# Attention and S4D layers on one core: kernel powers in ten double-buffered batches, scaled on GpSimd, with the step sizes first

## The chip, the cores and the metric

The kernel runs on one core of a Trainium2 chip. The metric is the device time of one execution in microseconds (us). A core has four compute engines that matter here: PE (TensorE, matrix products), DVE (VectorE), ACT (ScalarE) and POOL (GpSimd). SP (SyncE) issues most DMAs; POOL issues some. Each engine executes its own queue in order and waits on semaphores for the others.

## The reference

Four layers are applied to x (2048 tokens by 640 channels), alternately self-attention with 32 heads of 20 channels and a long convolution (S4D), each on the normalized x and added to it. Both attention layers share their weights, and so do both convolutions.

```
x = x + attention(layernorm(x), wqkv, wo)
x = x + s4d(layernorm(x), ...)
x = x + attention(layernorm(x), wqkv, wo)
x = x + s4d(layernorm(x), ...)

# the convolution kernel of s4d, for 640 channels d, 128 states n, 2048 positions l
dt = exp(log_dt)                              # the step sizes, one per channel
A  = -exp(log_A_real) + 1j * A_imag
C  = (C_real + 1j * C_imag) * dt[:, None]
P  = exp((A * dt[:, None])[:, :, None] * pos)
K  = 2 * einsum("dn,dnl->dl", C, P).real
y  = causal_convolution(u, K) + u * D_skip    # by FFT
```

## The kernel before

**Stages.** `seq` runs the layers. The first attention layer has two stages. A head stage (L664 to L748) loads the tokens in four groups of four blocks (`xr`), normalizes them (`ln_stats`, then L720 on ACT), transposes them on PE into two halves of half precision (`xh`, `xl`), and makes the first block of queries and keys (`block0`) and the first values (`values4`). Then the score loop (`scores`, `values`) runs 1024 times in a layer: PE computes a 128x1024 tile S (L769), ACT takes its exponential into `pt` (L772), and PE multiplies `pt` with the values V into `pa` (L786). The remaining queries, keys and values are computed beside it on PE (`jobs`, L560), and DVE empties the PSUM tiles `m` of those into `qc`. A plan with estimated costs (`Plan`, `slot`, `fill`, `weave`) decides while the program is written where each of these jobs stands between the scores.

**The convolution kernel.** `kgen` is a generator whose steps are woven into the first attention layer. It needs the powers of exp(A dt) at twelve exponents (LV, from 1 to 1536). First come the loads of `lar`, `aim`, `cr` and `ci` (128 states by 640 channels), then the step sizes: `ldt` is loaded as 128x5 (`k_d5`), `exp_exact` takes a polynomial exponential on DVE with one step on ACT, the result goes to DRAM (`dtd`) and comes back on all partitions (`k_dt`). `exp_exact` also runs on all of `lar` (128x640). DVE multiplies the four tiles by `k_dt`.

`powers(k)` then handles 128 channels, five times, in one set of the buffers `ks_`, `kc_` and `ke`. ACT makes 12 scaled copies of `aim` (L216); DVE reduces them to one turn and takes the absolute value (c); ACT takes two sines (L227, L229) and 12 exponentials of the scaled `lar` (L225); DVE multiplies cosine and sine by the exponential, and SP stores both to `wd` in DRAM. ACT must load another function table for a change between sine, exponential and square root; the order of the functions alternates between batches (`"esc"`, `"sce"`), so that like functions meet.

After the last batch `kgen` yields `"hold"`. Its second half gives the memory of the powers' buffers to new tiles (`ktab`, `kneg`), loads 32 channels of powers at a time back from `wd` (`kpw`, a DMA issued by POOL), expands them on DVE (`expand`, `left`, `right`), contracts them on PE (L322) and stores the kernel to `kd`.

**Order.** In the head stage a compile-time scheduler places the instructions: of those that are ready by its own estimates, each engine takes the one that was written first. The steps of `kgen` up to `"hold"` are written after the head stage, so they are placed where its work leaves an engine free. From the score loop on, `plan.keep` ties all matrix products, and the calls of DVE and the DMA issues of POOL and SP that go through `Ordered` (L74), to the order in which they are written. The engines execute the resulting queues in that fixed order. Nearly all of the calls on DVE, POOL and SP are recorded at line L74, that of the helper.

**Weights.** `stage` loads a slice of `wqkv` and returns `make`, which multiplies it by 256 and splits it into a half-precision part `wh` and its remainder `wl`, both on DVE. With `pool` given (the first block's weights `b0`, `b1` and the values' `b0`, `b1`, `b2`) it is used in the head stage. The second attention layer runs the same code with x already on the chip.

## Time and profile before

| what | us |
|---|---|
| median of 3 runs | 2904.78 (2903.93 to 2905.59) |
| profiled execution | 2906.51 |
| its span | 2904.6 |
| busy PE, ACT, DVE, POOL | 2581.2, 2360.6, 1497.7, 795.5 |
| first normalization on ACT (L720) | at 16.46 |
| first scaled copy of the powers (L216) | at 67.00 |
| first exponential of the scores (L772) | at 119.83 |
| second layer: first L720, first L772 | at 1606.27, at 1687.01 |

The profile records one execution. Times are in us from the start of its span. A line of a timeline has the start, the duration, the engine and the line of code, the operation, output and inputs with their shape, a count, and in brackets how long the engine had been idle before and what ended that. SPq and POOLq lines are DMA issues. A line of the stretches has the length, then the busy time of PE, of weight loads, DVE, ACT and POOL with the number of instructions, the granted clock of PE as a share of full speed, the DMA share and GB/s.

### The profile page before, as it was taken

To read this page: it belongs to the slowest core of one execution; us is meant where nothing else is said; L and a number is where in the kernel's file an instruction comes from. 1 tells how busy PE (TensorE), PEld (TensorE's weight loads), DVE (VectorE), ACT (ScalarE), POOL (GpSimd) and SP (SyncE) were. 2 spreads that over 40 slices of the span, in tenths; PEclk is the share of its full clock that TensorE was granted. 3 is DMA by queue.
4 is the path that set the end of the run, shared out by engine and by line. 5 is a ranking of instruction groups with operands and counts; after the bars stand their busy time and mean duration, and the time that the engine had idled before them with its cause. 6 is when DMAs were issued, how large, how long until landed. Compare 5 with 4: busy or idle time off the path is not lost.

```text
span 2904.6 us, 127995 instructions
## 1 busy us (share of the span) xinstructions
PE 2581.2 (89%) x57088; PEld 1537.6 (53%) x57088; DVE 1497.7 (52%) x3333; ACT 2360.6 (81%) x2862; POOL 795.5 (27%) x1229
## 2 busy tenths in 40 slices
PE   7679898998999788789999898999999978878999
PEld 3235555554555444367788554544444433334988
DVE  8555667777775687146777633332222200001865
ACT  5878888998899788855565488999999989998364
POOL 1002223222222222330067012222222332222376
PEclk9889999999999999999999999999999999999999
DMA  5212222222111111335454212121211211112265
GB/s 165 105 55 58 62 59 60 62 53 68 52 55 42 51 41 50 131 119 185 190 188 140 67 35 64 55 65 40 61 46 44 66 28 39 31 43 61 86 204 162
DMA packets 174754, 231.45 MB, mean 80 GB/s; under 512 B 35952, under 2 KB 124336, under 8 KB 172400
## 3 DMA queue, kind: packets, MB, share of 16 engines
q1 hardware_dynamic: 139856, 180.84, 19.2%
q0 software_dynamic: 34336, 42.32, 5.8%
q8 instruction: 450, 7.37, 1.1%
q14 instruction: 112, 0.92, 0.1%
HBM read 150.94 MB, written 72.10 MB: 77 GB/s over the span
## 4 chain that ended last, share of the span: by engine, by line
ACT 26%; PE 18%; issue 6%; DMA 3%; DVE 2%; POOL 1%; SPq 0%; ACTq 0%; POOLq 0%; DVEq 0%
ACT pt L772 25%; PE psv L1135 2%; PE psy L1145 2%; PE po L1041 2%; PE psx L1123 2%; PE psx L1100 2%; PE pst L1110 1%; PE pkf L1015 1%; PE pkx L998 1%; PE pv L524 1%; PE po L1035 1%; PE pa L786 1%; PE pq L682 1%; DMA kl<-kd 1%; PE pkt L1007 1%
## 5 line engine op out<-in xcount | busy, mean ns | idle before, releaser
L772 ACT ACTIVATE pt<-S 128x1024 f32<-128x1024 f32 x2048 | 1932.4, 1040 | 168.2 <-PE S L769 155.1
L786 PE MATMUL pa<-pt,V 64*32 64x512 f32 x16384 | 1144.3, 597 | 17.3 <-DVE oc L74 9.3
L769 PE MATMUL S<-qop,kop 61*32 61x512 f16 x16384 | 921.8, 383 | 184.6 <-ACT pt L772 149.1
L769 PEld LDWEIGHTS <-kop 61*32 61x32 f16 x16384 | 393.8, 90 | 836.9 <-issue 742.5
L786 PEld LDWEIGHTS pa<-pt,V 64*32 64x32 f32 x16384 | 330.1, 107 | 93.7 <-issue 32.0
L74 POOL DMA_DIRECT2D dn<-oc x256 | 126.2, 499 | 446.2 <-DVE oc L74 352.4
L74 POOL DMA_DIRECT2D ot<-oc x256 | 129.2, 512 | 392.5 <-DVE oc L74 313.3
L74 DVE TENSOR_SCALAR qc<-m 128x512 f32<-128x512 f32 x64 | 44.2, 690 | 298.9 <-PE m L560 298.8
L322 PE MATMUL m<-kb,ka 64*32 64x64 f32 x10240 | 158.4, 222 | 44.6 <-issue 42.4
L322 PEld LDWEIGHTS m<-kb,ka 64*32 64x32 f32 x10240 | 150.8, 105 | 82.4 <-issue 65.3
L74 DVE COPY oc<-pa 128x512 f32<-128x512 f32 x64 | 44.2, 691 | 275.0 <-PE pa L786 275.0
L74 POOL DMA_DIRECT2D db<-dn x256 | 128.5, 508 | 133.7 <-DMA dn<-dr 126.0
L74 DVE TENSOR_TENSOR kb<-ktab 128x512 f32<-128x512 f32 x240 | 155.9, 684 | 16.4 <-PE m L322 16.4
L560 PE MATMUL m<-xh,wh 64*32 64x512 f16 x2560 | 148.8, 382 | 12.5 <-DVE qc L74 12.5
L560 PE MATMUL m<-xl,wh 64*32 64x512 f16 x2560 | 148.0, 381 | 0.0
L560 PE MATMUL m<-xh,wl 64*32 64x512 f16 x2560 | 147.0, 380 | 0.2 <-issue 0.2
L560 PEld LDWEIGHTS <-wh 64*32 64x32 f16 x5120 | 97.1, 94 | 79.0 <-issue 42.2
L1128 POOL TENSOR_TENSOR t<-t,kb 128x512 f32<-128x512 f32 x80 | 101.9, 1274 | 71.2 <-DVE t L74 70.3
L1112 ACT COPY xt<-pst 128x1024 f16<-128x1024 f16 x80 | 81.6, 1023 | 46.7 <-PE pst L1110 46.5
L74 DVE TENSOR_SCALAR dr<-dr 128x16 f32<-128x16 f32 x64 | 14.7, 229 | 188.5 <-DMA dr<-dn 188.4
L74 DVE TENSOR_TENSOR oc<-oc,db 128x512 f32<-128x512 f32 x64 | 44.1, 690 | 125.7 <-DMA db<-dn 124.2
L74 POOL DMA_DIRECT2D dn<-dr x64 | 35.6, 556 | 263.8 <-DVE dr L74 256.7
(222 smaller groups left out, 3877.3 us busy)
## 6 DMA issues: line engine op xcount, KB each, us to landing
ka<-kha SPq DMA_DIRECT2D x80, 256.0 KB
kb<-khb SPq DMA_DIRECT2D x80, 256.0 KB
db<-dn POOLq DMA_DIRECT2D x256, 64.0 KB, 2.6
qop<-qs SPq DMA_DIRECT2D x256, 40.0 KB
kop<-ks SPq DMA_DIRECT2D x128, 80.0 KB
ot<-oc POOLq DMA_DIRECT2D x256, 40.0 KB, 2.0
otl<-ot SPq DMA_DIRECT2D x32, 320.0 KB
kha<-kn SPq DMA_DIRECT2D x20, 512.0 KB
```

Source lines behind the costliest of these rows:

```text
L74: made = f(out, *a, **k)
L322: chain(te.matmul(ps[r][32 * j:32 * j + 32, c8, :], a[n // 2][rows, ch, :], b[n][rows, dd, :], start=(n == 0), stop=(n == 3), tile_positio ...
L560: chain(te.matmul(ps[r][32 * t:32 * t + 32, :], a_[rows, ct, 32 * t:32 * t + 32], m[rows, ct, sl], start=(k == 0), stop=(k == 14), tile_po ...
L769: chain(te.matmul(S[32 * t:32 * t + 32, 512 * r:512 * r + 512], kt_[rows, kc + 32 * t:kc + 32 * t + 32], qt[rows, :], start=True, stop=Tru ...
L772: se.activation(pt, S, AF.Exp, scale=SCALE)
L786: chain(te.matmul(pa[r][32 * j:32 * j + 32, :], V[rows, kt, VP * h:VP * h + 32], pts[j // 2][rows, 512 * (j % 2):512 * (j % 2) + 512], sta ...
L1041: te.matmul(pos[hf], oh[:, ct, :], m[:, ct, 320 * hf:320 * hf + 320], start=False, stop=(ct == NCT - 1 and m is wol))
L1100: te.matmul(ps[:, r, i, :], e1[:, e, s, r, :], m[:, s, bs], start=(n == 0), stop=(n == 2))
L1112: se.copy(xt, pt.rearrange("p k g c -> p k (g c)"))
L1123: te.matmul(px, f2[:, f, :], xt[:, k, :], start=(n == 0), stop=(n == 2))
L1128: ge.tensor_mul(t2, t2, kb)
L1135: te.matmul(pv[:, g].rearrange("p r i c -> p (r i c)"), t1[:, g * P:g * P + P], fa, start=True, stop=True)
```

## The change

1. The step sizes' exponential, with its load and store, is written ahead of everything else, in a pool of its own; `kgen` only loads `k_dt`.
2. `lar`'s exponential is one ACT step in place of `exp_exact`.
3. `powers` handles 64 channels (BA), ten times, with two sets of buffers. The multiplications by the twelve exponents, for `aim` and now also for `lar`, run on POOL (24 of 128x64 a batch); ACT takes one wide exponential and two sines. `tie` keeps ACT's functions of successive batches in the written order.
4. `kpw` becomes two tiles of their own that do not reuse the powers' memory. The first two are loaded right behind batch 0, and later ones a batch further ahead.
5. In `stage`, `wh` of the head stage's weights moves from DVE to ACT, and the calls of `make` move behind the normalization of the first group.
6. The tokens of a group are loaded before the group ahead of it is handled; the first group's loads stand ahead of the weights', the selection matrix's behind them.

The core of the diff (the constants' lines and unchanged context are left out):

```
+    with tc.tile_pool(name="dt", bufs=1) as dp:
+        d5 = dp.tile([P, D // P], F32, name="k_d5")
+        sy.dma_start(d5, ldt.rearrange("o (p c) -> (o p) c", c=D // P))
+        exp_exact(dp, d5, D // P)
+        sy.dma_start(dtd.rearrange("o (p c) -> (o p) c", c=D // P), d5)
...
     def kgen():
-        BA, BC, DC = 128, 32, 8
+        BA, BC, DC = 64, 32, 8
...
+        kpw = [kp.tile([P, 2, BC, NL], F32, name=f"kpw{n}") for n in range(2)]
...
-            d5 = kx.tile([P, D // P], F32, name="k_d5")
-            sy.dma_start(d5, ldt.rearrange("o (p c) -> (o p) c", c=D // P))
-            exp_exact(kx, d5, D // P)
-            sy.dma_start(dtd.rearrange("o (p c) -> (o p) c", c=D // P), d5)
             sy.dma_start(dt, dtd.partition_broadcast(P))
             yield
-            exp_exact(kx, ld["lar"])
+            se.activation(ld["lar"], ld["lar"], AF.Exp)
...
-        kw1 = tc.tile_pool(name="kw1", bufs=1, side="right")
+        act = [None]
+        kw1 = tc.tile_pool(name="kw1", bufs=2, side="right")
...
             for n, v in enumerate(LV):
-                se.activation(s[:, :, n], ld["aim"][:, bs], AF.Copy, scale=v)
+                ge.tensor_scalar_mul(s[:, :, n], ld["aim"][:, bs], v)
+            for n, v in enumerate(LV):
+                ge.tensor_scalar_mul(e[:, :, n], ld["lar"][:, bs], v)
...
                 if f == "e":
-                    for n, v in enumerate(LV):
-                        se.activation(e[:, :, n], ld["lar"][:, bs], AF.Exp, scale=v)
+                    act[0] = tie(se.activation(e, e, AF.Exp), act[0])
                 elif f == "s":
-                    se.activation(s, s, AF.Sin, scale=TWO_PI)
+                    act[0] = tie(se.activation(s, s, AF.Sin, scale=TWO_PI), act[0])
                 else:
-                    se.activation(c, c, AF.Sin, scale=-TWO_PI, bias=hpi)
+                    act[0] = tie(se.activation(c, c, AF.Sin, scale=-TWO_PI, bias=hpi), act[0])
...
+            if k == 0:
+                for n in range(2):
+                    load_powers(n)
...
         def load_powers(k):
-            w = p2.tile([P, 2, BC, NL], F32, name="kpw")
-            ge.dma_start(w, wd[:, :, k * BC:k * BC + BC, :].rearrange("r p d n -> p r d n"))
-            return w
+            ge.dma_start(kpw[k % 2], wd[:, :, k * BC:k * BC + BC, :].rearrange("r p d n -> p r d n"))
...
-        cur = load_powers(0)
-        yield from expand(0, cur, tab, neg)
-        cur = load_powers(1)
+        yield from expand(0, kpw[0], tab, neg)
+        load_powers(2)
...
             if k + 1 < NE:
-                yield from expand(k + 1, cur, tab, neg)
-                if k + 2 < NE:
-                    cur = load_powers(k + 2)
+                yield from expand(k + 1, kpw[(k + 1) % 2], tab, neg)
+                if k + 3 < NE:
+                    load_powers(k + 3)
...
-                ve.tensor_scalar_mul(wh, wt, WS)
+                if pool:
+                    se.activation(wh, wt, AF.Copy, scale=WS)
+                else:
+                    ve.tensor_scalar_mul(wh, wt, WS)
...
+            coming = load_x(0)
             for i4 in range(4):
...
+                xr = coming
                 if i4 == 0:
+                    made_ = [stage(n * D, P, f"b{n}", wb[n], hp) for n in range(2)]
                     sy.dma_start(self_, c_sel)
-                    made_ = [stage(n * D, P, f"b{n}", wb[n], hp) for n in range(2)]
+                if i4 < 3:
+                    coming = load_x(i4 + 1)
...
-                if i4 == 0:
-                    for make in made_:
-                        make()
...
                     se.activation(t, xr[i], AF.Identity, scale=rs[:, i:i + 1], bias=nb[:, i:i + 1])
                     xn.append(t)
+                if i4 == 0:
+                    for make in made_:
+                        make()
```

More of the change, by code (lines that the diff above doesn't have):

```diff
@@ L156, in rstd, with exp_exact @@
         return rs
-    def exp_exact(pool, xx, n=D):
+    def exp_exact(pool, xx, n):
         k, r, q, z = (pool.tile([P, n], F32, name=f"ee_{t}{n}") for t in "krqz")
@@ L691, in values4, with load_x @@
                         pass
-            for i4 in range(4):
-                if x is None:
-                    xr = []
-                    for i in range(4):
-                        t = xp.tile([P, D], F32, tag=f"xr{i}", name=f"xr{i}")
-                        sy.dma_start(t, xv[:, 4 * i4 + i, :])
-                        xr.append(t)
-                else:
-                    xr = [x[:, 4 * i4 + i, :] for i in range(4)]
+            def load_x(i4):
+                if x is not None:
+                    return [x[:, 4 * i4 + i, :] for i in range(4)]
+                ts = [xp.tile([P, D], F32, tag=f"xr{i}", name=f"xr{i}") for i in range(4)]
+                for i, t in enumerate(ts):
+                    sy.dma_start(t, xv[:, 4 * i4 + i, :])
+                return ts
+            coming = load_x(0)
+            for i4 in range(4):
+                xr = coming
                 if i4 == 0:
+                    made_ = [stage(n * D, P, f"b{n}", wb[n], hp) for n in range(2)]
                     sy.dma_start(self_, c_sel)
-                    made_ = [stage(n * D, P, f"b{n}", wb[n], hp) for n in range(2)]
+                if i4 < 3:
+                    coming = load_x(i4 + 1)
                 if stats is None:
@@ L708, in attention @@
                     mv, rs = stats(i4)
-                if i4 == 0:
-                    for make in made_:
-                        make()
-                    made_ = [stage(2 * D + q * QW, QW, f"b{q}", [w[:, :, q * QW:q * QW + QW] for w in wv], hp)
-                             for q in range(NQ)]
-                    ve.tensor_copy(sel, self_)
                 xn = []
@@ L721, in attention @@
                     xn.append(t)
+                if i4 == 0:
+                    for make in made_:
+                        make()
+                    made_ = [stage(2 * D + q * QW, QW, f"b{q}", [w[:, :, q * QW:q * QW + QW] for w in wv], hp)
+                             for q in range(NQ)]
+                    ve.tensor_copy(sel, self_)
                 for ct in range(NCT):
```

## The prediction

> **What bounds the kernel now.** I read the page, then the busy time by stretches, then the timelines of ACT, DVE and SyncE up to 260 us, and last the same stage of the second attention layer, into which nothing else is woven.
>
> ```profile
> span 2904.6 us, 127995 instructions
> ...
> L772 ACT ACTIVATE pt<-S 128x1024 f32<-128x1024 f32 x2048 | 1932.4, 1040 | 168.2 <-PE S L769 155.1
> ```
>
> The exponentials on ACT (L772) pace both attention layers. They were kept waiting for 168.2 us in all, so it matters where that idle time lies.
>
> ```profile
> 118.50:175.60 57.10, 25.37 (x432) 9.23 (x432) 30.40 (x53) 40.28 (x76) 1.51 (x2) 0.67 0.25 95
> 175.60:250.00 74.40, 71.92 (x2099) 39.06 (x2090) 33.48 (x60) 73.77 (x79) 14.19 (x28) 1.00 0.14 42
> ```
>
> The columns are the length, then the busy time of PE, weight loads, DVE, ACT and POOL, then the granted clock. From 175.6 us ACT is busy 73.77 of 74.40 us. In the 57.1 us before, PE has 25.37 us of work at a granted clock of 0.67, and POOL has 1.51. The timeline of ACT tells what happens there:
>
> ```profile
> 16.46 3.36 ACT L720 ACTIVATE xr<-xr,nb,rs 128x640 f32<-128x640 f32 x4 [6.47 <-DVE nb L74]
> ...
> 67.00 0.66 ACT L216 ACTIVATE ks__1093<-k_aim 128x128 f32<-128x128 f32 x2 [1.40 <-DVE k_ci L74]
> ...
> 119.83 1.02 ACT L772 ACTIVATE pt<-S 128x1024 f32<-128x1024 f32 x1
> ...
> 173.77 1.02 ACT L772 ACTIVATE pt<-S 128x1024 f32<-128x1024 f32 x1 [13.90 <-PE S L769]
> 175.59 48.31 ACT L772 ACTIVATE pt<-S 128x1024 f32<-128x1024 f32 x51 [0.80 <-PE S L769]
> ```
>
> The first exponential runs at 119.83 us, and by 175.59 only 18 have run (the first and the last of them are shown). The last two batches of powers sit between them. Then DVE stops everything:
>
> ```profile
> 155.00 0.32 DVE L74 MEMSET ktab<- 128x96 f32 x2 [4.01 <-DMA wd<-kc__1236]
> 159.50 0.42 DVE L74 COPY ktab<-kpw 128x192 f32<-128x192 f32 x2 [4.19 <-DMA kpw<-wd]
> ...
> 170.21 0.68 DVE L74 TENSOR_SCALAR qc<-m 128x512 f32<-128x512 f32 x1
> ```
>
> In the loop DVE keeps the written order. It waits 4.01 us for the last store of the powers (wd), 4.19 us for the first load back (kpw), expands until 170.21, and only then empties the PSUM banks (qc) for which PE, and behind PE the scores, wait. So the powers set the start of steady running, not the attention's own preparation. The second layer shows that stage without them:
>
> ```profile
> 1606.27 4.17 ACT L720 ACTIVATE xn<-x,nb,rs 128x640 f32<-128x640 f32 x5
> ...
> 1674.45 0.30 ACT L530 ACTIVATE V<-pv 128x160 f32<-128x160 f32 x1 [1.73 <-DVE V L74]
> 1676.49 0.30 ACT L530 ACTIVATE V<-pv 128x160 f32<-128x160 f32 x1 [1.73 <-DVE V L74]
> ...
> 1687.01 33.60 ACT L772 ACTIVATE pt<-S 128x1024 f32<-128x1024 f32 x36 [0.78 <-DMA qop<-qs]
> ```
>
> There 36 exponentials take 33.60 us (0.933 each) from the very first. Eighteen would take 16.8 us, so the 19th, now at 175.59, could run at 119.83 + 16.8 = 136.6: the loop holds 39.0 us of stall. The stage ahead has slack too: from normalization to first exponential it takes 1687.01 - 1606.27 = 80.7 us there and 119.83 - 16.46 = 103.4 us here. Part of that is more work: a token block's values take 1676.49 - 1674.45 = 2.04 us there for 320 columns; for the first layer's 480 I estimate 3.06, over 16 blocks 16 us more. The other 103.4 - 80.7 - 16 = 6.7 us are disturbance.
>
> **The change, part by part.** *Head of the stage.* Between the root of the variance and nb, DVE casts weights:
>
> ```profile
> 9.78 0.20 ACT L150 ACTIVATE lt<-va 128x4 f32<-128x4 f32 x1 [7.76 <-DVE va L74]
> ...
> 16.27 0.15 DVE L74 SCALAR_TENSOR_TENSOR nb<-mv,rs 128x4 f32<-128x4 f32 x1
> ```
>
> The root is there at 9.98. Six small steps of some 0.15 us with nothing between would bring nb to 10.9, 5.4 us earlier. The step sizes' exponential now runs first: 17 DVE steps of five columns, at most 17 x 0.15 = 2.6 us, part of it before the first tokens land; I charge 1.4. Its load and store stand ahead of later loads on SyncE's queue; if the store's wait holds tokens up, the lower bound below covers it. So 4 us are won, with bounds 0 and 6. Five casts go from DVE to ACT, behind the normalization; two of them precede the first q and k products, which I leave inside these bounds. The tokens a group ahead I cost at nothing: their buffers are double already, and what covers them is the matrix work of the group before. Of the 6.7 us of disturbance I take 3 as gone (bounds 0 and 7), since twelve long DVE steps of the exact exponential leave the stage. First exponential: 119.8 - 7 = 113, bounds 107 and 120.
>
> *Start of the powers.* They need the step sizes on all partitions (k_dt), and lar and aim:
>
> ```profile
> 15.95 0.63 SPq L74 DMA_DIRECT2D k_aim<-in_aim  x1
> ...
> 59.77 0.32 SPq L74 DMA_DIRECT2D k_dt<-dtd  x1
> ```
>
> k_dt is loaded at 59.77, and the first scale runs at 67.00. With that chain done near 10 us, what is late next is lar and aim, issued at about 16, and two DVE steps that give way to the layer's own work. With some 4 us to land (the wait after the last wd store is of that size) and as much again until DVE is free, POOL could begin at 25; I take 29, with bounds 22 and 67 (nothing won).
>
> *Length of the powers.* Now 67.00 to 155.00: 88 us for five batches, 17.6 each. The prices:
>
> ```profile
> L225 ACT ACTIVATE ke<-k_lar 128x128 f32<-128x128 f32 x60 | 16.1, 432 | 0.4 <-DVE kc__1128 L74 0.4
> ...
> L227 ACT ACT_TABLE_LOAD x5 | 6.4, 1283 | 3.3 <-DVE kc__1128 L74 1.9 <-DVE kc__1236 L74 1.0 <-DVE kc__1164 L74 0.4
> ...
> L227 ACT ACTIVATE ks__1093<-ks__1093 128x1536 f32<-128x1536 f32 x1 | 1.5, 1484 | 0.0
> ```
>
> Per 128 channels ACT now runs 24 narrow steps (16.1 / 60 = 0.268 each, as they overlap), 6.4 us, then two sines of 1.5 and two table loads of 1.28: 12.0 us. After it: three wide passes, 4.5 us cut in two with a little overhead, 4.9, and again two table loads, since one batch's order is sines first and the next one's exponential first: 7.5 us. That frees 22 us of ACT over the five. Here the Trainium skill speaks against smaller batches: "ScalarE: Activation LUTs", section What ACT_TABLE_LOAD costs, puts a switch of set at 2.66 us, a drain included. By that the ten switches would cost 27 us and not 13, but every switch in this trace shows the load of 1.283 and the next step right behind, so I go by the row.
>
> POOL gets 24 multiplications of 128x64 per batch, 240 in all, written at a stride. No POOL row is that step; the nearest are:
>
> ```profile
> L925 POOL CAST woh<-wot 128x640 fp32r<-128x640 f32 x10 | 7.0, 715 | 6.9 <-DMA wot<-in_wo 5.4 <-DMA qop<-qs 1.5
> ...
> L74 POOL MEMSET V<- 128x128 f32 x6 | 2.1, 344 | 0.0
> ```
>
> Ten times the columns take 0.715, and twice the elements, strided, 0.344. I take 0.25 us, nearest to the second, with bounds 0.1 and 0.7. At 0.25 a pair of batches has 12 us of POOL, beside the other engines, as the second set of buffers lets POOL run one batch ahead. The pair's period is then the chain of one buffer: half the POOL work of a batch (3), reduction on DVE (2), ACT (5), products (2), store (4), 16 us if nothing queues and two batches share it. With the layer's own work in between I take 17, and 5 x 17 = 85 us. ACT has the room:
>
> ```profile
> 1606.00:1720.00 114.00, 103.19 (x1312) 62.21 (x1316) 57.00 (x129) 71.87 (x109) 2.64 (x5) 0.97 0.20 58
> ```
>
> Of these 71.87 us, 33 are exponentials, so the stage's own share of ACT is 39 us; with wider values and five casts some 48, of which about 10 lie before 29 us. From 29 to 113 that leaves 84 - 38 = 46 us for 5 x 7.5 = 38. So the powers end at 29 + 85 + 4 for the last store = 118, bounds 105 and 160, and the last batch or so falls beside the first exponentials.
>
> *Into the loop.* kpw has buffers of its own and is loaded after batch 0, so the 4.19 us go; the multiplications queued behind these two loads on POOL wait for a store (4 us, one time), covered by the batch already scaled. From memset to steady running it was 175.59 - 155.00 = 20.6, less 4.2 leaves 16.4. Powers: 118 + 16.4 = 134.4. Attention: 113 + 16.8 = 129.8. The later one holds: the 19th exponential comes at 134.4 instead of 175.6, 41 us earlier. Behind it the written order is the same, and the loads a batch further ahead only widen a cover that is there (kpw is waited for once). In the second layer the same casts move from DVE to ACT and behind the normalization, which ACT did first there already: nothing, bounds -2 and +2. I take 2 off for steps that the in-order queues hold up, and get 39.
>
> Sum: 2904.6 - 39 = 2865.6 of span; the profiled execution took 2906.51 against a span of 2904.6, and the median is 2904.78, so 2866 stands for the median.
>
> **The rivals.** *The powers still trail into the loop.* If queues of three engines in fixed order leave three of ten batches at the first exponential, each costs there what two batches of twice the size cost between 119.83 and 155.00, 35 us, by four: 8.8 us. 113 + 26 + 4 + 16.4 = 159.4, a gain of 16: 2889. For it speaks that ACT has only 46 - 38 = 8 us to spare.
>
> *The start does not move.* If k_dt's load stays where it is on SyncE's queue, the powers run from 67 for 85 us, end at 152 + 4, and the loaded kpw alone is won: 3 us and 7 from the head that nobody waits for. 2902, within 0.2%, about what a measurement of this kernel can tell from no change. Against it: nothing of the layer stands ahead of that chain any more.
>
> *POOL becomes the bound.* 240 steps of p from 29 us, and 12 behind for the last batch: the break-even is 29 + 240 p + 12 = 159, at p = 0.49 us. At 0.65, as for a step whose cost is all fixed, the end is 197, the 19th exponential at 213, and the time 2904.8 + 38 = 2943. A steady theft of POOL's port by DVE would do it as well:
>
> ```profile
> L1128 POOL TENSOR_TENSOR t<-t,kb x80: 1264/1274/1284, 1469.7 to 2886.2; 128x512 f32<-128x512 f32 x80
> ```
>
> All 80 stay within 1264 and 1284 ns beside a working DVE, so I see no theft. The Trainium skill, "GPSIMD Engine Reference", section Key points, has DVE steps with two SBUF inputs contend with GpSimd, which would be this case.
>
> **How the numbers follow.** Forecast 0.62; trailing powers 0.17; start unmoved 0.07; POOL as the bound 0.08; better than forecast 0.06 (powers by 105, first exponential by 107, 19th at 124: 2853). Faster takes the forecast, the trailing and the better case, and a third of the unmoved start: 0.87. Within 0.2%: 0.05. Slower: 0.08. The range goes from 2850, below the better case, to 2892, past the trailing one, and leaves out the last two rivals.
>
> **What would show it.** Right: in the changed profile the first POOL multiplication lies at 25 to 35 us and takes 0.2 to 0.35; the first L772 lies at 107 to 118; the memset of ktab does not wait past 120; the copy from kpw waits for no DMA; L772's idle time falls by over 20 us, and PE's clock is full from 120 on. Wrong: POOL busy without a gap up to the memset, an exponential still followed by 14 us of idle ACT, or a first normalization later than 16.

## The result, and the profile after

The changed kernel takes 2952.25 us (median of 4 runs, 2950.21 to 2955.98) against 2904.36 us of the kernel before on the same chip: a ratio of 1.0163, 95% interval 1.015 to 1.0176. It is slower by 48 us, where 39 us of gain were forecast. The profiled execution has a span of 2950.8 us, 46.2 more than before. The page after:

```profile
span 2950.8 us, 128213 instructions
...
PE 2584.5 (88%) x57088; PEld 1538.6 (52%) x57088; DVE 1483.2 (50%) x3334; ACT 2350.8 (80%) x2773; POOL 904.7 (31%) x1469
...
L785 ACT ACTIVATE pt<-S 128x1024 f32<-128x1024 f32 x2048 | 1932.9, 1040 | 156.9 <-PE S L782 143.6
```

The exponentials are now at L785. They take what they took (1932.9 us) and wait 156.9 us instead of 168.2. So the score loop lost nothing; the loss lies ahead of it. ACT's timeline at the same places as before:

```profile
18.14 3.35 ACT L727 ACTIVATE xr<-xr,nb,rs 128x640 f32<-128x640 f32 x4 [5.49 <-DVE nb L74]
...
203.15 2.85 ACT L785 ACTIVATE pt<-S 128x1024 f32<-128x1024 f32 x3
207.05 1.02 ACT L785 ACTIVATE pt<-S 128x1024 f32<-128x1024 f32 x1 [1.05 <-PE S L782]
208.57 22.46 ACT L785 ACTIVATE pt<-S 128x1024 f32<-128x1024 f32 x24 [0.49 <-PE S L782]
```

The first exponential runs at 203.15 us, 83.3 later than before. From there the loop runs nearly without a hole: the 19th is the 15th of the 24 that begin at 208.57, so it starts at 208.57 + 14 x 0.936 = 221.7, which is 46.1 after the 175.59 of before. That is the whole difference of the spans. DVE at the start of the kernel's second half:

```profile
205.64 0.14 DVE L74 MEMSET ktab<- 128x96 f32 x1 [2.70 <-DMA wd<-kc__1414]
205.80 0.25 DVE L74 COPY ktab<-kpw 128x192 f32<-128x192 f32 x1
...
216.54 0.68 DVE L74 TENSOR_SCALAR qc<-m 128x512 f32<-128x512 f32 x1
```

The copy from `kpw` waits for no DMA, as forecast, and the first `qc` comes 10.9 us behind the memset instead of 15.2. But the memset, which waits for the last store of the powers, runs at 205.64 instead of 155.00. POOL's timeline tells what the powers were waiting for:

```profile
47.46 5.42 POOL L220 TENSOR_SCALAR ks__1080<-k_aim 128x64 f32<-128x64 f32 x12 [24.50 <-DVE k_ci L74]
52.96 6.09 POOL L222 TENSOR_SCALAR ke<-k_lar 128x64 f32<-128x64 f32 x12
...
79.78 7.05 POOL L222 TENSOR_SCALAR ke<-k_lar 128x64 f32<-128x64 f32 x12 [8.48 <-DVE ks__1080 L74]
...
153.87 4.98 POOL L220 TENSOR_SCALAR ks__1341<-k_aim 128x64 f32<-128x64 f32 x12
164.84 0.44 POOL L74 PARTITION_ALL_REDUCE k2m<-k  x1 [5.99 <-issue]
172.45 0.47 POOL L222 TENSOR_SCALAR ke<-k_lar 128x64 f32<-128x64 f32 x1 [7.17 <-issue]
...
190.87 7.11 POOL L222 TENSOR_SCALAR ke<-k_lar 128x64 f32<-128x64 f32 x12
```

Each line is a run of up to twelve multiplications. It begins at 47.46 (29 forecast), takes 5.0 to 7.1 us per twelve (3.0 forecast), and ends at 197.98. The 240 steps fill 116.7 us of these 150.5. Of the rest, 4.3 us are POOL's two loads of `kpw`, its transfers of `qm` and the all-reduce; 15.5 us are three waits for a buffer that DVE still uses (8.48 is shown, the others are 2.67 and 4.33); and 13.2 us stand around the all-reduce with nothing to wait for ("issue", 5.99 and 7.17). On the other side of the hand-over, DVE stands at the first step that reads a set:

```profile
64.14 0.56 DVE L74 TENSOR_SCALAR kc__1118<-ks__1119 128x768 f32<-128x768 f32 x1 [9.03 <-POOL ks__1119 L220]
123.97 0.56 DVE L74 TENSOR_SCALAR kc__1229<-ks__1230 128x768 f32<-128x768 f32 x1 [9.15 <-POOL ks__1230 L220]
180.15 0.56 DVE L74 TENSOR_SCALAR kc__1377<-ks__1378 128x768 f32<-128x768 f32 x1 [10.50 <-POOL ks__1378 L220]
```

There are ten such waits, one per batch, of 4.55 to 10.50 us, 72.5 us in all. DVE's queue is in order, so the layer's own work stands behind them, and PE behind that: one of ACT's copies into V follows 18.58 us of idle time, ended by DVE's, and from 170 to 200 us PE is busy 1.19 of 30 us at a granted clock of 0.50 (the figure behind the length, and the one behind POOL's count):

```profile
159.71 0.30 ACT L538 ACTIVATE V<-pv 128x160 f32<-128x160 f32 x1 [18.58 <-DVE V L74]
```
```profile
170.00:200.00 30.00, 1.19 (x16) 0.54 (x17) 6.02 (x8) 5.94 (x7) 23.76 (x52) 0.50 0.15 55
```

### The profile page after: what moved, and what is told of

Same layout as the page of the kernel before. It is cut to its first block, busy times and chain, and to the rows that moved or that the text cites. A ratio compares the mean times of both kernels' runs of the same rounds, so it can differ in the third digit from the quotient of the medians.

```text
span 2950.8 us, 128213 instructions
## 1 busy us (share of the span) xinstructions
PE 2584.5 (88%) x57088; PEld 1538.6 (52%) x57088; DVE 1483.2 (50%) x3334; ACT 2350.8 (80%) x2773; POOL 904.7 (31%) x1469
## 4 chain that ended last, share of the span: by engine, by line
ACT 24%; PE 20%; issue 5%; DMA 2%; DVE 2%; POOL 1%; SPq 0%; POOLq 0%; ACTq 0%; DVEq 0%
ACT pt L785 23%; PE psv L1148 2%; PE psy L1158 2%; PE psx L1136 2%; PE pa L799 2%; PE psx L1113 2%; PE po L1054 2%; PE pv L532 1%; PE pst L1123 1%; PE pkf L1028 1%; PE S L782 1%; PE pkx L1011 1%; PE pq L690 1%; PE po L1048 1%; DMA kl<-kd 1%
## 5 line engine op out<-in xcount | busy, mean ns | idle before, releaser
L785 ACT ACTIVATE pt<-S 128x1024 f32<-128x1024 f32 x2048 | 1932.9, 1040 | 156.9 <-PE S L782 143.6
L74 DVE TENSOR_TENSOR kb<-ktab 128x512 f32<-128x512 f32 x240 | 155.6, 681 | 16.4 <-PE m L328 16.4
L532 PE MATMUL pv<-wv,xh 128*128 128x480 f16 (+1 forms) x320 | 86.1, 357 | 42.8 <-DVE V L74 36.3
L532 PEld LDWEIGHTS <-xh 128*128 128x128 f16 x800 | 70.1, 100 | 92.9 <-issue 71.7
```

Source lines behind the costliest of these rows:

```text
L74: made = f(out, *a, **k)
L532: chain(te.matmul(ps[:, :n], a_[:, ct, sl], m[:, ct, :], start=(k == 0), stop=(k == 14)))
L785: se.activation(pt, S, AF.Exp, scale=SCALE)
```

## The experiments

The first theory read these rows as a matter of order: a compile-time queue that puts DVE's read of a set, and POOL's all-reduce behind the sets, ahead of the attention's own preparation. Its rivals were the amount of POOL's work, whatever the order, and steps of POOL and DVE that slow each other. Fourteen kernels were run. This table collects them. They ran on several chips, so the ratio, which is to the kernel before on the same chip, compares them better than the medians do; the memset is that of `ktab`, and the last column is the span of the profiled execution less the time of the memset.

| kernel | median us | ratio (95%) | first exponential | memset | span - memset |
|---|---|---|---|---|---|
| before | 2904.36 | 1 | 119.83 | 155.00 | 2749.6 |
| after | 2952.25 | 1.0163 (1.015 to 1.0176) | 203.15 | 205.64 | 2745.2 |
| act_scales | 2894.51 | 0.9966 (0.9954 to 0.9979) | 120.88 | 154.29 | 2744.7 |
| pool_alone | 2970.96 | 1.0213 (1.0192 to 1.0234) | 167.21 | 222.18 | 2748.2 |
| head_alone | 2892.19 | 0.9964 (0.9949 to 0.998) | 121.16 | 141.50 | 2743.5 |
| dve_alone | 2894.01 | 0.9969 (0.9958 to 0.998) | 117.39 | 147.56 | 2743.7 |
| dve_wide | 2878.81 | 0.9914 (0.99 to 0.9928) | 122.39 | 138.55 | 2738.4 |
| dve_wide_oldhead | 2880.70 | 0.992 (0.9906 to 0.9935) | | | |
| pool_wide | 2898.72 | 0.9981 (0.9971 to 0.999) | 153.06 | 155.55 | 2741.3 |
| pool_idle_work | 2961.52 | 1.0199 (1.0182 to 1.0216) | 189.90 | 223.31 | 2732.8 |
| pool_idle_four | 2906.48 | 0.9998 (0.9986 to 1.0011) | 128.42 | 161.82 | 2746.0 |
| order_tied | 2944.51 | 1.0143 (1.0102 to 1.0185) | 138.48 | 201.15 | 2742.2 |
| pool_half | 2936.30 | 1.0099 (1.0068 to 1.0129) | 147.45 | 191.76 | 2746.0 |
| no_all_reduce | 2938.26 | 1.0106 (1.0085 to 1.0126) | 173.12 | 200.09 | 2742.4 |
| pool_half_three | 2918.17 | 1.0047 (1.003 to 1.0064) | 135.26 | 168.15 | 2746.5 |
| after_early | 2944.64 | 1.0126 (1.0108 to 1.0144) | 197.51 | 200.00 | 2738.8 |

The last column is the main finding. The memset moves over a range of 85 us, and what follows it stays between 2738 and 2750 us, but for one kernel. The first exponential shows no such tie: order_tied has it 65 us earlier than the changed kernel, and the intervals of their ratios overlap. The end of the powers sets the time, and everything below asks what sets the end of the powers. Of dve_wide_oldhead only the times are used.

### Which part of the change costs: act_scales, pool_alone, head_alone

act_scales is the changed kernel with the scalings back on ACT; all else stays.

```
-                ge.tensor_scalar_mul(s[:, :, n], ld["aim"][:, bs], v)
-            for n, v in enumerate(LV):
-                ge.tensor_scalar_mul(e[:, :, n], ld["lar"][:, bs], v)
+                se.activation(s[:, :, n], ld["aim"][:, bs], AF.Copy, scale=v)
...
-                    act[0] = tie(se.activation(e, e, AF.Exp), act[0])
+                    for n, v in enumerate(LV):
+                        act[0] = tie(se.activation(e[:, :, n], ld["lar"][:, bs], AF.Exp, scale=v), act[0])
```

> The changed kernel with the twelve scaled copies and twelve scaled exponentials of a batch back on ACT, as before; all else as changed. Theory 1 (DVE's fixed queue waits for POOL's 5 us of multiplications, 72 us of such waits in the changed trace, with the layer's own evacuations queued behind): those waits go, the first exponential comes at 110 to 130 instead of 203, and the time falls to 2865 to 2905. Theory 2 (ten batches hand over between engines twice as often, whoever multiplies): the head stage stays over 170 us and the time over 2930.

As the first theory expected, it is faster than the kernel before, 0.9966, and 58 us faster than the changed one. The rest of the change is worth a little, and POOL's scalings cost all of the loss. Its powers go at the pace of ACT, which is busy 27.4 of the 30 us from 100 to 130; a pair of batches takes 20.8 us in the mean (from 50.20 to 154.29 for five).

pool_alone is the opposite: the kernel before, with its five batches and one set of buffers, and only the scalings on POOL (128x128 steps).

> The kernel before with one thing changed: the 24 multiplications of each of the five batches on POOL, 128x128 each, and one wide exponential. Theory 1: slower than before by 30 us or more, since a batch now has 24 POOL steps of over 0.42 us in its one chain (over 10 us a batch, 50 in all, less the 30 us of ACT that they free). Theory 2 (the number of batches is the cost): within 10 us of before.

```profile
67.41 7.58 POOL L216 TENSOR_SCALAR ks__1093<-k_aim 128x128 f32<-128x128 f32 x12 [54.05 <-DVE k_ci L74]
75.08 10.12 POOL L218 TENSOR_SCALAR ke<-k_lar 128x128 f32<-128x128 f32 x12
```

It loses 2.1%. Twelve steps of twice the columns take 7.58 us at their fastest, 0.63 each, where 64 columns take 0.42: so I estimate some 0.2 us fixed and 3 ns per column. With one set of buffers POOL also waits four times, 9.78 to 13.78 us, until a buffer is given back.

head_alone is the kernel before with the parts 1, 2, 5 and 6 of the change, and the powers as they were.

> The kernel before with the head's parts alone: step sizes first, lar by one ACT step, casts on ACT behind the normalization, tokens a group ahead; the powers in five batches scaled by ACT, loaded back where they were. The prediction's head (4 us earlier, powers from 29): 2870 to 2890. By the changed trace (first normalization at 18.1, not 12; k_dt used at 34): powers start some 15 us earlier and the first tokens 2 us later, 2885 to 2902. If the new order of the head costs more than that: 2905 or over.

It gains 0.4%, inside its second expectation and short of the first, which took the prediction's head. The powers start at 49.79 instead of 67.00 and the memset moves to 141.50. Its first normalization lies at 18.07, so the later start of the head that the changed kernel shows is made here, and costs nothing that the end sees.

### POOL's time, or steps that slow each other: pool_idle_work, pool_idle_four, pool_wide

pool_idle_work is act_scales plus the same 240 multiplications on POOL into a tile that nobody reads.

```
+            for r in range(2):
+                for n, v in enumerate(LV):
+                    ge.tensor_scalar_mul(e2[:, :, n], ld["aim" if r else "lar"][:, bs], v)
```

> As act_scales, and in addition POOL makes the same 24 multiplications a batch into a tile that nobody reads (work added that the output does not need). Theory 1 (it is the waiting for POOL): within 5 us of act_scales. Theory 3 (POOL's work itself slows DVE, or its queue delays the reduction of the key lengths): slower than act_scales by over 10 us.

It was far slower, against the first theory's number. Its trace gives the reason: DVE waits once, 69.1 us, for the all-reduce, which the compiled queue of POOL has behind all the multiplications:

```profile
54.95 5.11 POOL L224 TENSOR_SCALAR ke<-k_aim 128x64 f32<-128x64 f32 x12
60.15 7.96 POOL L224 TENSOR_SCALAR ke<-k_lar 128x64 f32<-128x64 f32 x12
...
103.68 5.37 POOL L224 TENSOR_SCALAR ke<-k_lar 128x64 f32<-128x64 f32 x12
109.13 5.09 POOL L224 TENSOR_SCALAR ke<-k_aim 128x64 f32<-128x64 f32 x12
...
174.16 0.37 POOL L74 PARTITION_ALL_REDUCE k2m<-k  x1 [6.67 <-issue]
```

While DVE waits, twelve steps take 5.08 us; while it works, mostly 6.4 to 8.0. The exception is the set at 54.95, 5.11 us: there ACT is busy throughout, and DVE first waits and then subtracts `xh` from a PSUM tile, so that only one of its inputs lies in SBUF. So it is DVE that slows POOL here, not ACT, and not with every step. pool_idle_four keeps that and takes the queue away: the dummy steps are there for the first four batches alone (`range(2 if k < 4 else 0)`), and end before the all-reduce.

> The changed kernel with scalings on ScalarE, and the same GpSimd multiplications into a tile that nobody reads, for batches 0 to 3 alone (96 steps, some 43 us of GpSimd between 45 and 100 us, while VectorE works on the head, done before the all-reduce). It tells the queue order from the shared port. Theory 1: nobody waits for these steps, the all-reduce is not behind them; time within 5 us of the 2894.5 of the same kernel without them (2888 to 2901), first exponential at 118 to 126; VectorE's own steps may show a longer mean. Rival B (the port): VectorE loses what GpSimd's steps take from it; 96 of 240 steps of a loss of 67 us give 27 us: 2912 to 2930, first exponential past 135.

```profile
98.01 6.67 POOL L224 TENSOR_SCALAR ke<-k_aim 128x64 f32<-128x64 f32 x12
104.74 1.57 POOL L74 DMA_DIRECT2D kpw<-wd  x2
113.03 0.37 POOL L74 PARTITION_ALL_REDUCE k2m<-k  x1 [6.72 <-issue]
```

2906.48 us lies between the two expectations, 0.3% above act_scales by the ratios, and neither theory had it. Two things make its memset 7.5 us later (together they come to 8.4). The maxima that the all-reduce reads end at 107.24 (104.56 in act_scales): 2.7 us of slowing under 54 us of POOL's steps. And the all-reduce runs 5.8 us after them, behind 6.72 us of idle time; in act_scales it runs 0.1 us after them. So slowing costs DVE little, and there is a cost of changing POOL from multiplications to the all-reduce that no theory had.

pool_wide takes two steps per batch instead of 24: a 768-wide product of two broadcast operands on POOL.

```
...
+            for t, n in ((s, "aim"), (e, "lar")):
+                ge.tensor_mul(t, ld[n][:, bs].unsqueeze(2).to_broadcast(shp), lvt.unsqueeze(1).to_broadcast(shp))
```

> The changed kernel with POOL's 24 multiplications of 64 columns a batch made as two of 768 columns, by a broadcast operand of the twelve exponents. From the 512-column two-input row of before (1274 ns) I work out 1.9 us for one, 3.8 a batch in place of 10. Theory 1: the waits on POOL shrink from 5 to 2 us for a set, the time falls to 2870 to 2910. Theory 2: over 2930. Theory 3 (a POOL step with two inputs and DVE's two-input steps hold each other up): POOL's step takes over 2.5 us and DVE's products over 1.1.

```profile
99.70 1.94 POOL L222 TENSOR_TENSOR ks__1144<-k_aim,lvt 128x768 f32<-128x768 f32 x1
101.60 1.50 POOL L222 TENSOR_TENSOR ks__1159<-k_aim,lvt 128x768 f32<-128x768 f32 x1
```
```profile
101.68 1.84 DVE L74 TENSOR_SCALAR kc__1143<-ks__1144 128x768 f32<-128x768 f32 x1 [1.39 <-POOL ks__1144 L222]
```

The same products take POOL 1.5 to 1.95 us in place of 5 to 7, and the kernel goes from 1.0163 to 0.9981, inside the first expectation. Buffers, pairs and the two gaps around the all-reduce (5.91 and 6.78 us here) are as in the changed kernel. So POOL can scale without loss against the kernel before if its price is a third. DVE's step at 101.68 takes 1.84 us instead of 0.56 and ends at 103.52, 0.42 after POOL's step: it seems to have been held for all of that.

### The order of the queues: order_tied

The instructions of the changed kernel, with ties that put DVE's and ACT's powers behind V's copies of certain token tiles, and POOL's batches 5 to 9 behind the all-reduce and `qm`. The core of it:

```
+    AFTER = {0: 2, 1: 3, 2: 6, 3: 7, 4: 11, 5: 13}
...
+                if k >= 5:
+                    behind(o, qmd[0])
...
+            behind(o, evd[AFTER.get(k, 15)])
+            if k >= 1:
+                behind(o, nbs[3])
```

> The changed kernel with the same instructions on the same engines; only the order on the queues is tied: the angle reduction of batch 0, 1, 2, 3, 4, 5 stands behind VectorE's copy of V's token tile 2, 3, 6, 7, 11, 13 (of 16), later batches' behind tile 15, ScalarE's powers likewise, and GpSimd's scalings of batches 5 to 9 behind the all-reduce and the four transfers of qm. Theory 1 (the loss is VectorE and GpSimd holding the layer's own head behind scalings that are not ready): the head runs as it does without GpSimd's scalings, the all-reduce lies at 100 to 112 us, the first loop exponential at 115 to 128 instead of 203.15; GpSimd still needs 10.5 to 13 us a batch, so the powers end at 160 to 180 us and trail into the loop; time 2895 to 2925. Rival A (GpSimd's amount of work sets the end, whatever the order): 240 steps end where they did, 19th exponential near 222, time 2945 to 2955. Rival B (steps slowing each other at the shared memory port): the same overlap of the same steps, so the first exponential stays past 170 and the time over 2935.

```profile
125.93 0.37 POOL L74 PARTITION_ALL_REDUCE k2m<-k  x1 [5.77 <-issue]
127.66 2.28 POOL L74 DMA_DIRECT2D qm<-mr  x4 [1.35 <-DVE V L74]
137.69 5.06 POOL L228 TENSOR_SCALAR ks__1267<-k_aim 128x64 f32<-128x64 f32 x12 [7.76 <-DMA kop<-ks]
```
```profile
138.48 2.86 ACT L807 ACTIVATE pt<-S 128x1024 f32<-128x1024 f32 x3 [0.68 <-PE S L804]
162.99 2.83 ACT L807 ACTIVATE pt<-S 128x1024 f32<-128x1024 f32 x3
173.93 1.94 ACT L807 ACTIVATE pt<-S 128x1024 f32<-128x1024 f32 x2
```

The first theory falls here. The head is free again (first exponential at 138.48; 115 to 128 was expected), but the time is 2944.51, next to the range of the rival that had POOL's amount of work set the end, and the 19th exponential runs at 217.71, 4.0 us earlier than in the changed kernel. The ratios, 1.0143 (1.0102 to 1.0185) and 1.0163 (1.015 to 1.0176), do not tell the two kernels apart. The queues give the reason: by 201.15, where the memset runs, only 11 exponentials have run, since the rest stand on ACT's queue behind the last batches' powers. Sixty-five us won in the head were stall in the loop.

### How much of it is POOL's amount: pool_half, pool_half_three

pool_half scales the angles alone on POOL (120 steps); ACT keeps its twelve exponentials.

> The changed kernel with the angle scalings alone on GpSimd (120 steps); ScalarE keeps its twelve exponentials with a scale per batch. Theory 1 (a wait appears only where a batch's scalings take GpSimd longer than the other engines' pace): a set takes 5 to 6.5 us against 9 us of pace per batch seen with the scalings on ScalarE, so VectorE's waits for the scaled angles fall from 72.5 us to under 20, the first loop exponential comes at 116 to 130, and the time is 2880 to 2900. Rival B (each GpSimd step costs the others something, in proportion to their number): half the loss over the kernel with ScalarE's scalings stays, 2894.5 + 29 = 2923, between 2912 and 2935.

```profile
84.14 5.06 POOL L220 TENSOR_SCALAR ks__1154<-k_aim 128x64 f32<-128x64 f32 x12
89.27 6.02 POOL L220 TENSOR_SCALAR ks__1190<-k_aim 128x64 f32<-128x64 f32 x12
113.96 5.39 POOL L220 TENSOR_SCALAR ks__1226<-k_aim 128x64 f32<-128x64 f32 x12 [18.67 <-DMA wd<-ks__1154]
...
168.83 5.85 POOL L220 TENSOR_SCALAR ks__1370<-k_aim 128x64 f32<-128x64 f32 x12 [11.80 <-DMA wd<-ks__1298]
```

2936.30 was above both expectations as they were written. Its ratio of 1.0099 is 2933 us on the chip of the changed kernel, the upper end of rival B's range, so this time alone does not rule rival B out. DVE's waits for the angles came to 45 us, where under 20 were expected. POOL is busy 59 of the 160 us from 40 to 200 and still holds the powers, and the rows say how: it scales two batches, then waits 18.67 and 11.80 us until their transfers to `wd` have given the two buffers back. ACT takes batches in pairs, so one pair fills both sets of buffers, and POOL's 11 us stand in a row with DVE, ACT and the store instead of beside them. Pairs begin at 49.98, 84.14, 113.96, 145.88 and 168.83.

pool_half_three adds a third buffer for the scaled angles and keeps the order of POOL's queue.

```
-            s = p1.tile(shp, F32, name="ks_")
+            s = p1.tile(shp, F32, name="ks_", bufs=3)
...
+                if k >= 6:
+                    tie(o, qmd[0])
```

> The kernel with the angle scalings alone on GpSimd, and a third buffer for the scaled angles; GpSimd's queue has the same order as there. Theory: with two buffers a pair of batches fills both, so GpSimd can't start on the next pair until the pair's transfers to wd have landed, and its 11.5 us stand in a row with the reductions, the powers on ScalarE and the transfers; the rounds between the first scalings of pairs were 34, 30, 32 and 23 us there, with 18.67, 0.82 and 11.80 us of GpSimd's waits for wd. A third buffer lets the first half of the next pair run ahead: some 5 us less in each of the rounds, first loop exponential at 130 to 142 instead of 147.45, time 2912 to 2926 against 2936. Rival (GpSimd's steps slow VectorE and ScalarE, or the order on VectorE's queue holds the head, whatever the buffers): within 6 us of 2936.

```profile
126.67 5.06 POOL L222 TENSOR_SCALAR ks__1298<-k_aim 128x64 f32<-128x64 f32 x12 [7.27 <-issue]
...
149.81 6.48 POOL L222 TENSOR_SCALAR ks__1406<-k_aim 128x64 f32<-128x64 f32 x12 [5.59 <-DMA wd<-ks__1298]
```

As expected: 2918.17 us, the first exponential at 135.26, the memset 23.6 us earlier than in pool_half. The ratio falls from 1.0099 to 1.0047, some 15 us, with intervals that just do not overlap, and the number of steps is the same. The two buffers were a cause there. More than three were not tried.

### The change-over and the late start: no_all_reduce, after_early

no_all_reduce is the changed kernel with a copy on DVE in place of the first layer's all-reduce.

> The changed kernel with the first layer's all-reduce left out: VectorE copies k2 to k2m, so that the maximum over the 128 partitions isn't taken there (the shift under the softmax differs from row to row; the same matmuls and exponentials run). Theory: on GpSimd a change from the multiplications to the all-reduce and back costs time by itself, since an extra instruction stands ahead of each; the changed kernel shows 5.99 us of idle before the all-reduce and 7.17 us after it with nothing to wait for, and GpSimd is what the powers wait for there. Without the all-reduce both gaps go: GpSimd's last scaling ends 10 to 14 us earlier than 197.98, and the time is 2936 to 2945 against 2952. Rival: the gaps are waits for data that the profile does not show (the maxima, or a buffer); then they stay somewhere else, GpSimd's last scaling ends within 4 us of 198, and the time is within 5 us of 2952.

```profile
161.44 2.16 POOL L74 DMA_DIRECT2D qm<-mr  x4 [1.58 <-DVE k2m L74]
168.57 6.05 POOL L222 TENSOR_SCALAR ke<-k_lar 128x64 f32<-128x64 f32 x12 [4.97 <-DVE ks__1304 L74]
```

Both gaps are gone, and the time is 2938.26, as expected; by the memset it gains 5.5 us, by the spans 8.3, by the medians 14, so its size is known no better than that. POOL's last scaling ends at 191.06, 6.9 us earlier and not the 10 to 14 expected, for a wait of 4.97 us for a buffer stands in the place of the gaps. The trace of the changed kernel has, on POOL's own queue, what stands in the gaps: a change of its configuration at 158.9, ahead of the all-reduce at 164.84, and another at 165.2, ahead of the multiplication at 172.45.

```profile
L74 POOLq MODIFY_POOL_CONFIG  x2: 16/16/16, 158.9 to 158.9; - x2
```
```profile
L222 POOLq MODIFY_POOL_CONFIG  x2: 83/83/83, 165.2 to 165.3; - x2
```

The last figures are the first and the last start. From each it takes 5.9 and 7.1 us until POOL works again. The kernel before has the first of them too, at 13.3 us, but there POOL has nothing to do in the 90 us ahead of the all-reduce, and no second one comes in this stage:

```profile
103.26 0.38 POOL L74 PARTITION_ALL_REDUCE k2m<-k  x1 [90.24 <-DVE k L74]
```

after_early puts `k_dt` in the pool of `k_lar`, so that the powers' buffers don't take its memory.

```
-            dt = kx.tile([P, D], F32, name="k_dt")
+            dt = klp.tile([P, D], F32, name="k_dt")
```

> The changed kernel with k_dt in the pool of k_lar and k_aim instead of one of its own, so that the buffers of the powers don't take over k_dt's place; everything else is the same. Theory: the first multiplication on GpSimd waits for k_ci's scaling at 46.56 us only because the scaled angles lie where k_dt lay, which that scaling still reads; with k_dt elsewhere GpSimd starts behind k_lar's and k_aim's scalings, at 35 to 38 us instead of 47.46, and runs the two decay sets first. The end of the powers sets the time (span less the time of ktab's memset is 2738 to 2750 us in nearly all kernels so far), and GpSimd sets their end: part of the 11 us goes over, as the third decay set still waits for a buffer; memset at 194 to 202 us instead of 205.64, time 2938 to 2949 against 2952. Rival (GpSimd's start comes from the queue's order or from the transfers, not from the place of k_dt): first multiplication within 2 us of 47.5, time within 3 us of 2952.

```profile
35.19 11.98 POOL L222 TENSOR_SCALAR ke<-k_lar 128x64 f32<-128x64 f32 x24 [12.38 <-DVE k_lar L74]
...
74.19 6.86 POOL L222 TENSOR_SCALAR ke<-k_lar 128x64 f32<-128x64 f32 x12 [15.20 <-DVE ks__1080 L74]
```

POOL starts at 35.19 instead of 47.46, and the time is 2944.64, as expected. The wait "for k_ci" in the changed kernel was for memory: the scaled angles lie where `k_dt` lay, and `k_ci`'s scaling at 46.56 is the last to read it. Of the 12 us, 5.6 reach the memset; the third decay set waits 15.20 us for a buffer instead of 8.48.

### DVE scales: dve_alone, dve_wide, dve_wide_oldhead

The two wide products of pool_wide, on DVE: in the kernel before (dve_alone, 1536 wide), in the changed kernel (dve_wide), and in the latter with the head's casts and token loads as before (dve_wide_oldhead).

```
...
+            for t, n in ((s, "aim"), (e, "lar")):
+                ve.tensor_mul(t, ld[n][:, bs].unsqueeze(2).to_broadcast(shp), lvt.unsqueeze(1).to_broadcast(shp))
```

> The kernel before with one thing changed: a batch's scaling as two DVE steps of 1536 columns and one wide exponential; five batches, one set of buffers. ACT loses 120 narrow steps (32 us) and gains five of 1.5 us. If ACT's load sets the length: the powers end 15 to 25 us earlier, 2880 to 2890. If the chain of one buffer does: under 8 us, 2897 to 2905.

> The changed kernel with the scaling on DVE, two steps of 768 columns a batch by a broadcast operand. Against act_scales, where ACT is busy 101 of 110 us from 50 to 160, it takes 240 narrow steps of 0.16 us (38 us) off ACT and adds 20 of 0.95 us (19 us) to DVE. If ACT's load now sets the length of the powers, they end near 125 instead of 154 and the time is 2865 to 2880. If the hand-over of ten batches between engines sets it (some 19 us a pair, whoever scales), they end at 145 or later and the time is 2885 to 2900.

> As dve_wide, with the head's tokens, casts and their place as before the change (the step sizes stay first, lar stays one ACT step). If the rearranged head costs time (first normalization at 18.1 against 16.5): 2 to 8 us less than dve_wide. If it pays: 2 to 8 us more.

```profile
50.10 0.95 DVE L74 TENSOR_TENSOR ks__1082<-k_aim,lvt 128x768 f32<-128x768 f32 x1
...
138.55 0.14 DVE L74 MEMSET ktab<- 128x96 f32 x1 [2.71 <-DMA wd<-kc__1218]
```

dve_wide beats both kernels: 2878.81 us, 0.9914 (0.99 to 0.9928), inside its first expectation; the memset at 138.55 lies between the ends that its two expectations gave. A wide step takes DVE 0.95 us, so a batch costs 1.9 us there in place of 10 to 14 on POOL and of 24 narrow steps on ACT. A pair of batches takes 17.7 us (from 50.10 to 138.55 for five, the last store included), near the 17 that the prediction had. dve_alone gains 0.3%, between its two expectations: its first copy from `kpw` still waits 4.19 us. dve_wide_oldhead is equal to dve_wide within the intervals, so parts 5 and 6 of the change are neutral there.

## Why the prediction was wrong

**What bounds the kernel: right.** The powers set the start of steady running, and the table shows it for nearly every kernel. The forecast's own sum has 2866 us for powers that end at 118; 2866 - 118 = 2748 is in the table's range. With 205.6 for the 118, the same sum gives 2953. All of the error is in the end of the powers.

**Into the loop: right.** The wait at `kpw` is gone, and from the memset to the 19th exponential it takes 16.1 us; 16.4 was forecast. The second layer takes 79.0 us from its first normalization to its first exponential (1652.68 to 1731.66) against 80.7, inside the forecast's 2.

**Head: wrong, with little effect.** The first normalization came at 18.14 and not near 12. The first halves of the weights' split left DVE, but their remainders still ran ahead of it, at 12.01 and 15.68 us with 0.82 each, and the step sizes' chain and the statistics of the next group, whose tokens now come earlier, took the rest of the place on DVE: the reciprocal runs at 15.00 us, with the root there at 12.03. The root itself is 2.05 us later than the 9.98 of before: the step sizes' exponential and a table load of 1.28 us stand ahead of it on ACT, which the prediction did not charge. The first exponential, forecast at 113, came at 203.15; order_tied has it at 138.48 and is not clearly faster than the changed kernel, so little of the loss hangs on that.

**Start of the powers: wrong by 18.5 us**, 47.46 for 29, inside bounds of 22 to 67. The step sizes did come early (`k_dt` was loaded at 26.38 instead of 59.77), but the step said "two DVE steps that give way to the layer's own work" and counted two readers of `k_dt` out of four. The others held the memory of the first scaled buffer. after_early won 12 us of the start.

**Length of the powers: the step that failed.** "I take 0.25 us, nearest to the second" failed first: the step takes 0.424 us beside a waiting DVE, and 116.7 us / 240 = 0.486 with DVE at work. So POOL needed 116.7 us where 60 were forecast. pool_wide shows that this term decides: it lowers POOL's price and keeps the rest, and the loss is gone. The row that was taken wrote constants; a step that also reads 64 columns has the fixed part that pool_alone suggests. The value lay between the bounds, 0.1 and 0.7. The term "as the second set of buffers lets POOL run one batch ahead" failed next. The batches go in pairs, a pair holds both sets, and POOL can't run ahead into the next pair: pool_half and pool_half_three show it with half the steps, and in the changed kernel POOL's waits for buffers are 15.5 us. The third part was in no step of the prediction: two change-overs around the all-reduce, 13.2 us in the changed kernel. no_all_reduce shows that they are real and part of the loss. The Trainium skill has the price, and the prediction passed over it: "GPSIMD Engine Reference", section Instruction dispatch, says that the first call after new code is loaded to GpSimd costs about 6 us more. The 5.99 us ahead of the all-reduce agree; the way back is somewhat dearer here, 7.17.

**The rival that came true** had a chance of 0.08: POOL as the bound. With its own formula and the measured start and price, 47.5 + 116.7 + 12 = 176 for 159 is 17 us later, 2922. The waits for buffers (15.5) and the change-overs (13.2) add 28.7: 2951, against 2952 measured. That it comes so near is partly luck: the sum leaves out the 4.3 us of POOL's other work, and the 12 us behind the last step measured 7.7 (197.98 to 205.64). Its break-even of 0.49 us was for a start at 29. For 47.5 it is (159 - 47.5 - 12) / 240 = 0.41, just under the 0.424 beside a waiting DVE, so two errors that each lay within their bounds met.

**Contention: dismissed too early.** The row of the second convolution (1264 to 1284 ns) showed POOL at a steady pace, not POOL without disturbance. In this stage its steps go from 424 up to 1172 ns. The Trainium skill, "GPSIMD Engine Reference", section Key points, says that some of DVE's steps contend with GpSimd, and the traces agree: twelve steps take 5.08 us beside a waiting DVE and mostly 6.4 to 8.0 beside a working one. By 240 x 0.424 = 102 us I estimate this at some 15 of the 116.7; its effect on DVE, 2.7 us in pool_idle_four, is the smaller part.

What stays open: order_tied and no_all_reduce were not run together, and the third buffer not with all 240 steps on POOL, so how the parts of the loss add up is worked out and not measured.

## What to carry to other kernels

Find the one event behind which the rest runs unchanged, here the memset that ends the powers, and price every part of a change by what it does to that event. Work moved to an idle engine is a new link in the chain: it takes the new engine's price per step, it runs ahead only if a whole group of buffers is free (two buffers and work in pairs are one buffer), and what that engine did before, here one all-reduce, now waits behind it. Where a narrow step is repeated with a scalar, look first whether one wide step with a broadcast operand on the engine that reads the result is cheaper: 1.9 us on DVE did what took POOL 10 to 14.

## What the runs showed of the hardware

- A one-input multiplication of 128x64 on POOL, written at a stride of twelve, takes 0.424 us beside a waiting DVE, of 128x128 0.63 us in the mean of the quickest twelve. A product of 128x768 with two broadcast operands takes POOL 1.50 us and DVE 0.95 us.
- POOL idles 5.5 to 6.7 us ahead of an all-reduce that follows multiplications and whose data are there, and 6.8 to 7.8 us ahead of the multiplication that follows it. In before, act_scales, head_alone, dve_alone and dve_wide, which have no multiplications on POOL at that place, the all-reduce runs 0.1 to 0.2 us after its data.
- Beside POOL's steps DVE's mean durations hardly move (the copies into V take 314 ns, and 319 without POOL's work), but single steps do: 0.56 us became 1.84 beside a wide product on POOL.
